# Value loads through one fp32 buffer, one early q/k load from ScalarE's queue, and three pairs' transposes in other PSUM banks

## The chip, the cores and the metric

The kernel runs on one core of a Trainium2 chip. The metric is the time of one execution on the device, in microseconds (us); lower is better. Engines are called PE (TensorE, matmul), DVE (VectorE), ACT (ScalarE), POOL (GpSimd) and SP (SyncE, which here only issues DMAs).

## What is computed

Attention with a window of 96 keys and 8 global keys, an ALiBi bias and softmax, and after it a mixer that adds a low-rank mixing along the sequence and a feed-forward block. Cut to what matters:

```python
scores = q @ k.T / sqrt(D) + bias            # B=4, H=8, S=768, D=64
scores = where(is_global | is_local, scores, -1e9)
a = softmax(scores)
x = concat_heads(a @ v)                      # (4, 768, 512)
h = (x.T @ U @ V).T                          # along the sequence, rank 32
u = x + h
out = u + relu(u @ w_ch1) @ w_ch2            # 512 -> 2048 -> 512
```

## The kernel before, in words

**The tiles.** The heads are worked on in pairs: 4 pairs a batch (`NP` = 4), 16 pairs in all (`NPAIR`), numbered 0 to 15 here. A pair's q, k and v are loaded in fp32 (384 KB each) into the staging tiles qst, kst and vst, two buffers each (L94, L119), cast to fp16 by an engine (`cast_qk`, L108; `cast_v`, L125, on POOL), and used from there. Pairs 0 to 7 (`NPE` = 8) have q and k transposed by PE (`st_T`, L229: twelve 128x128 transposes into two PSUM tiles named tp), and copied out by ACT (two halves of q, into qz) and DVE (k, into kT). Pairs 8 to 15 have them transposed by DMA (`turn`, L308). The rows of pairs 0 to 7 are read from memory in stretches of 1536 bytes (L96), those of the other pairs (L101) and of all values (L120) in stretches of 256 bytes.

**The stages of a pair.** Scores in three chunks (`st_SE` for batch 0, `st_S` after it), exponentials on ACT, the product with the values (`st_V`, once for each head of the pair), whose result DVE divides into x_sb (L427) and POOL casts to fp16, x16 (L428). Then the low-rank mixing: `st_M1` (L437 for batches after the first) multiplies x16 of a pair with U and needs the casts of both heads; `st_MT`, `st_M3` and a DMA transpose (`st_X`, L480) follow.

**Feed-forward.** For each half of a batch there are 16 up units (L526, `mk_up`: four matmuls into a PSUM tile hps, which ACT empties into htr, L530) and down units (L546, `mk_down`: four matmuls each into a tile cps). They stand in two queues, and `fill(n)` puts the next n of them between the attention steps of the pairs, so that PE has work while attention waits. No down unit is placed before the loop's i = 7 (L678, `held`). The first weights w1 come in four chunks (`load_w1`), the second, w2, in four (`load_w2`), issued by POOL, which casts them to fp16 during the DMA.

**PSUM.** Eight banks: tag th (three banks, for hps, tp, ups and tmp_ps), tag cps (two, for the down units; in batch 0 also for scores, and for the output of pair 3's second head), tag sc (two) and tag ob (one). Up unit 0 is begun early in a cps bank (L662).

**Order.** Everything is ordered by hand (`manual_schedule`, L138): each engine does its instructions in the order in which the code gives them, and waits are by semaphore. SP issues all loads but the weights, all stores and all DMA transposes, in one in-order queue; its next DMA waits until the one before it could be issued, and an issue waits until its target buffer is free. Batch 0 is the loop at L615; the rest is the loop at L674, whose pass i does scores of pair i, values and division of pair i-1, and transposes and casts ahead. In the second loop SP's loads stand at L683 to L690: q/k of a later pair, then the values of pair i+1, ahead of the cast of values i (L697) and of `st_A` (L698, which for pairs 8 to 15 issues the two vA DMAs, L289 and L290). On POOL the order in pass 5 is: `cast_v`, `st_A`, w2 chunk 2 (L700), L428 for pair 4's second head, w2 chunk 3 (L708).

**Activation memory.** htr (L523) has two buffers of 128 x 16 x 384 fp16; they are first written when the up units begin, after batch 0.

Of the kernel before, what the change touches and what calls it, by code (L numbers as in the profile page):

```python
# [11 lines left out]
FP32 = mybir.dt.float32  # L12
FP16 = mybir.dt.float16
# [7 lines left out]
def kernel(  # L21
# [13 lines left out]
    nc = tc.nc  # L35
    B, H, S, D = q.shape
    NG = int(n_global)
    NL = int(n_local)
    P = 128
    DM = H * D  # L40
    NSB = S // P
    DFF = moe_w_ch1.shape[1]
    NDC = DM // P
    NJC = DFF // P
    R = moe_U.shape[1]
    NP = H // 2
# [14 lines left out]
    GT = S // 2  # L61
# [4 lines left out]
    stp = ctx.enter_context(tc.tile_pool(name="stp", bufs=2))  # L66
# [4 lines left out]
    ffp = ctx.enter_context(tc.tile_pool(name="ffp", bufs=2))  # L71
    psum = ctx.enter_context(tc.tile_pool(name="psum", bufs=1, space=bass.MemoryType.PSUM))
# [10 lines left out]
    def ps_th(name, dtype=FP32, cols=512):  # L83
        return psum.tile([P, cols], dtype, name=name, tag="th", bufs=3)
# [2 lines left out]
    NVB = 4  # L87
    vbuf = [cst.tile([P, NSB, 2, D + 1], FP16, name=f"v16_{i}") for i in range(NVB)]

    def load_qk(i):  # L90
        b, h0 = i // NP, 2 * (i % NP)
        got = []
        for src, nm in ((q, "qst"), (k, "kst")):
            st = stp.tile([P, 2, NSB, D], FP32, name=nm, tag=nm, bufs=2)  # L94
            if i < NPE:
                nc.sync.dma_start(  # L96
                    st.rearrange("p h n d -> p h (n d)"),
                    src[b, h0:h0 + 2].rearrange("h (p n) d -> p h (n d)", n=NSB),
                )
            else:  # L100
                nc.sync.dma_start(  # L101
                    st.rearrange("p h n d -> p (h n) d"),
                    src[b, h0:h0 + 2].rearrange("h (n p) d -> p (h n) d", p=P),
                )
            got.append(st)
        staged[i] = got
# [9 lines left out]

    def load_v(i):
        b, h0 = i // NP, 2 * (i % NP)
        st = stp.tile([P, 2 * NSB, D], FP32, name="vst", tag="vst", bufs=2)  # L119
        nc.sync.dma_start(  # L120
            st, v[b, h0:h0 + 2].rearrange("h (n p) d -> p (h n) d", p=P)
        )
        vsts[i] = st
# [9 lines left out]
    NPAIR = B * NP  # L133
# [48 lines left out]
    def finish_table(t):  # L182
        nc.gpsimd.tensor_scalar_max(t[0:NG, 0, 0:P], relB[0:NG, 0:P], float(-NL))
        nc.gpsimd.memset(t[0:NG, :, P:], float(-NL))
# [29 lines left out]
    def load_w2(c):  # L214
        nc.gpsimd.dma_start(w2_16[:, 4 * c:4 * c + 4], w2v[:, 4 * c:4 * c + 4])
# [13 lines left out]
    def st_T(i):  # L229
        stq, stk = cast.pop(i)  # L230
        kT = kp.tile([P, S], FP16, name="kT", tag="kT")
        kA = kp.tile([P, NSB - 1, P], FP16, name="kA", tag="kA")
        tps = []
        for st in (stq, stk):

            tp = ps_th("tp", FP16, S)
            tps.append(tp.rearrange("d (n p) -> d p n", n=NSB))
            for n in range(NSB):
                nc.tensor.matmul(
                    tp[:, n * P:(n + 1) * P], st[:, n].rearrange("s h d -> s (h d)"), ident16,  # L240
                    is_transpose=True, start=(n == 0), stop=(n == NSB - 1),
                )
        tq, tk = tps
        z = qz[i % 2]
        if i == 0:
            kts[i], kas[i] = kT, kA
            for a in range(2):
                ts, ps = slice(a * GT, (a + 1) * GT), slice(a * P // 2, (a + 1) * P // 2)
                for hi in range(2):
                    r = slice(hi * D, (hi + 1) * D)  # L250
                    nc.scalar.copy(
                        z[hi][r, ts].rearrange("d (p n) -> d p n", n=NSB), tq[r, ps]
                    )
                nc.vector.tensor_copy(kT[:, ts].rearrange("d (p n) -> d p n", n=NSB), tk[:, ps])
                ns = slice(0, 2) if a == 0 else slice(2, NSB - 1)
                nc.vector.tensor_copy(
                    kA[:, ns].rearrange("d n p -> d (n p)"), kT[:, ns.start * P:ns.stop * P]
                )
                ns = slice(max(1, ns.start), ns.stop)
                nc.vector.tensor_copy(  # L260
                    kA[:, ns, 0:NG],
                    kT[:, 0:NG].unsqueeze(1).broadcast_to((P, ns.stop - ns.start, NG)),
                )
            return
        nc.scalar.copy(z[0][0:D].rearrange("d (p n) -> d p n", n=NSB), tq[0:D])
        nc.vector.tensor_copy(kT.rearrange("d (p n) -> d p n", n=NSB), tk)  # L266
        kts[i], kas[i] = kT, kA
        if i > NP:
            st_KA(i, nc.gpsimd)
        if i <= NP + 1:  # L270
            nc.scalar.copy(z[1][D:P].rearrange("d (p n) -> d p n", n=NSB), tq[D:P])
        else:
            nc.vector.tensor_copy(z[1][D:P].rearrange("d (p n) -> d p n", n=NSB), tq[D:P])

    def st_KA(i, eng):
        kT, kA = kts[i], kas[i]
        eng.tensor_copy(kA.rearrange("d n p -> d (n p)"), kT[:, 0:S - P])
        eng.tensor_copy(  # L278
            kA[:, 1:, 0:NG], kT[:, 0:NG].unsqueeze(1).broadcast_to((P, NSB - 2, NG))
        )  # L280
# [334 lines left out]
    for i in range(NP):  # L615
        st_SE(i, 0)
        if i:
            st_V(i - 1, 0)
        cast_v(i)
        st_A(i)  # L620
        if i < 2:
            load_v(i + 2)
        if i in (1, 2):
            load_qk(NP - 1 + i)
        if i == 2:
            load_w1(0)
        if i == 3:
            load_v(NP)
        if i >= 2:
            st_M1(i - 2)  # L630
        if i:
            st_T(i + 1)
        st_SE(i, 1)
        if i:
            st_V(i - 1, 1)
        else:
            st_T(i + 1)
        st_KA(i + 1, nc.vector)
        st_P(i)
        if i == 2:  # L640
            st_M2(i - 2)
        if i == 0:
            cast_qk(i + 2, nc.vector, nc.gpsimd)
        elif i < 3:
            cast_qk(i + 2, nc.gpsimd)
        if i == 2:
            load_w1(1)
        if i == 3:
            load_w1(2)
            load_w1(3)  # L650
        st_SE(i, 2)
        if i == 3:
            st_M2(i - 2)
# [4 lines left out]
    cast_qk(NP + 1, nc.gpsimd)  # L658
    st_M2(NP - 2)
    nc.scalar.copy(relcat, rel3)  # L660
    finish_table(relcat)
    begin_up(0, (0, 1), ps_cps("hps"))  # L662
    st_M1(NP - 1)
# [10 lines left out]
    for i in range(NP, NPAIR + 2):  # L674
        b, hp = divmod(i, NP)
        live = i < NPAIR
        n = 1 if i < 2 * NP + 1 else 2
        held[0] = i < NP + 3  # L678
        if hp == 0 and live and b + 1 < B:
            new_batch(b + 1)  # L680
        if live and i > NP:
            st_S(i, 0)
        early = {NP: (NP + 2,), NP + 1: (NP + 3,), NP + 2: (NP + 5,)}  # L683
        for j in early.get(i, (i + 3,)):
            if j < NPAIR:
                load_qk(j)
        if i + 1 < NPAIR:
            load_v(i + 1)
        if i == NP + 1:
            load_qk(NP + 4)  # L690
        fill(2)
        if NP < i <= NPAIR:
            st_V(i - 1, 0)
        if i + 1 < NPE:
            st_T(i + 1)
        if live:
            cast_v(i)  # L697
            st_A(i)  # L698
            if i == NP + 1:
                load_w2(2)  # L700
        fill(n)
        if live:
            st_S(i, 1)
        fill(1)
        if NP < i <= NPAIR:
            st_V(i - 1, 1)
        if i == NP + 1:
            load_w2(3)  # L708
        if i > NP + 1 and (i - 2) % NP == NP - 1:
            queue_ff((i - 2) // NP, 0)  # L710
            queue_ff((i - 2) // NP, 1)
            ahead[0] = 1
        if i == NPAIR + 1:
            break
        more = 1 if i + 1 < NPE else 0
        fill(n + more)
        if live:
            st_S(i, 2)
            if i < NPE:
                st_P(i)  # L720
        fill(1)
        if i > NP:
            st_M1(i - 1)
        if NPE <= i + 1 < NPAIR:
            st_Z(i + 1)
        if i + 2 < NPAIR:
            cast_qk(i + 2, nc.gpsimd)
        if i == NP:
            load_w2(0)
            load_w2(1)  # L730
        if live:
            st_E(i, 0)
        fill(1)
        if i > NP:
            st_MT(i - 1)
        if NPE <= i + 1 < NPAIR:
            st_K(i + 1)
        fill(1)
        if i > NP:
            st_M3(i - 1, 0)  # L740
        if live:
            st_E(i, 1)
        fill(1)
        if i > NP:
            st_M3(i - 1, 1)
            st_X(i - 1)
        if i + 2 < NPAIR and i + 2 >= NPE:
            turn(i + 2)
        fill(n - more)
# [38 lines left out]
```

## Time and profile before

| what | value |
|---|---|
| median of 3 runs | 239.45 us (239.22 to 239.78) |
| the profiled execution | 239.77 us |
| its span, first to last instruction | 238.0 us |
| granted TensorE clock | 1.00 |
| PE busy | 227.8 us (96%) |
| DVE, ACT, POOL busy | 130.2, 120.7, 94.9 us |
| HBM read, written | 27.46 MB, 6.29 MB |

How to read it: the profile is of one execution. Each engine's busy time is the sum of its instructions; the idle time before an instruction is put down to whoever ended it. Matmuls are pipelined and overlap, so PE's gaps are best seen from start to start: six 128-column matmuls in a row start about 0.055 us apart, four 384-column ones 0.163 us. The DMA share is that of 16 DMA engines; a DMA is moved as packets, here one for each stretch of memory. The loads' median time from issue to landing is 4.9 us (q), 5.5 (k), 6.1 (v), and 10.8 for a weight chunk.

### The profile page before, as it was taken

The numbers are of one execution on the slowest core, as the hardware profiler recorded it, in microseconds if no ns is written. First come the engines' busy times: TensorE is split into PE (matmuls) and PEld (weight loads), VectorE is DVE, ScalarE is ACT, GpSimd is POOL, SyncE is SP. The second block draws the span as 40 slices with busy tenths as digits, with TensorE's granted clock in tenths as the row PEclk, the third lists the DMA queues.
The fourth block names the chain that finished last, engine by engine and source line by source line (L and its number), as shares of the span: only waits on it lengthen the run. The fifth ranks groups of instructions, "written<-read, shape, count | busy, mean of one in ns | idle before, by whom it ended". The sixth has DMA issues, their size and how long they took to land.

```text
span 238.0 us, 4939 instructions
## 1 busy us (share of the span) xinstructions
PE 227.8 (96%) x1964; PEld 139.2 (59%) x1964; DVE 130.2 (55%) x281; ACT 120.7 (51%) x207; POOL 94.9 (40%) x146
## 2 busy tenths in 40 slices
PE   7889969999999999999999999999999999999994
PEld 2558746757555556666666566666555555555453
DVE  4777656789687786665766775755333111011121
ACT  6989767786741302865544317473632244533200
POOL 8479937576474635455727254513111000000000
PEclk9999999999999999999999999999999999999999
DMA  6999999999978989997969581751211210011022
GB/s 191 308 284 280 240 232 236 245 230 164 212 167 213 221 237 165 254 169 182 214 167 222 170 232 42 204 29 39 69 55 38 85 47 25 19 44 47 13 75 88
DMA packets 86558, 36.61 MB, mean 154 GB/s; under 512 B 74152, under 2 KB 83592, under 8 KB 86536
## 3 DMA queue, kind: packets, MB, share of 16 engines
q1 hardware_dynamic: 81480, 32.01, 56.1%
q0 software_dynamic: 5056, 4.29, 11.5%
q8 instruction: 15, 0.25, 0.4%
q14 instruction: 7, 0.06, 0.1%
HBM read 27.46 MB, written 6.29 MB: 142 GB/s over the span
## 4 chain that ended last, share of the span: by engine, by line
PE 78%; DMA 7%; DVE 5%; POOL 4%; ACT 2%; issue 1%; SPq 1%; POOLq 0%
PE cps L546 33%; PE hps L526 30%; DMA w<-in_moe_w_ch_dram 4%; DMA kst<-in_k_dram 3%; PE sc L349 3%; PE sc L354 2%; PE ob L408 2%; PE cps L564 1%; PE ob L404 1%; DVE kT L266 1%; POOL v L127 1%; DVE x_sb L427 1%; ACT ep L392 1%; PE sc L491 1%; POOL x L428 1%
## 5 line engine op out<-in xcount | busy, mean ns | idle before, releaser
L530 ACT ACTIVATE htr<-hps 128x384 f16<-128x384 f32 x128 | 61.3, 492 | 84.0 <-PE hps L526 83.4
L526 PE MATMUL hps<-uT,w 128*128 128x384 f16 x506 | 97.5, 326 | 0.7 <-DVE uT L473 0.3
L546 PE MATMUL cps<-w,htr 128*128 128x512 f16 x368 | 91.2, 379 | 0.0
L526 PEld LDWEIGHTS <-w 128*128 128x128 f16 x506 | 46.5, 98 | 29.4 <-issue 1.0
L380 DVE SCALAR_TENSOR_TENSOR sp<-sc,relcat 128x512 f32<-128x512 f32 (+1 forms) x72 | 43.2, 640 | 20.2 <-PE sc L354 14.3
L546 PEld LDWEIGHTS <-htr 128*128 128x128 f16 x368 | 34.1, 98 | 31.1
L552 DVE TENSOR_TENSOR osb<-cps,x_sb 128x512 f32<-128x512 f32 x23 | 15.9, 690 | 49.8 <-PE cps L546 49.5
L392 ACT ACTIVATE ep<-sp 128x1408 f16<-128x1408 f32 x24 | 32.7, 1372 | 12.2 <-DVE sp L380 12.2
L428 POOL CAST x<-x_sb 128x384 f16<-128x384 f32 x30 | 15.5, 518 | 49.5 <-DVE x_sb L427 49.4
L349 PE MATMUL sc<-qz,kT 128*128 128x128 f16 x192 | 27.8, 219 | 0.2 <-DVE kT L266 0.2
L354 PE MATMUL sc<-qz,kA 128*128 128x128 f16 x160 | 25.5, 220 | 0.9 <-DVE kA L278 0.3
L349 PEld LDWEIGHTS <-kT 128*128 128x128 f16 x192 | 18.3, 98 | 3.9 <-DVE kT L266 0.5
L354 PEld LDWEIGHTS <-kA 128*128 128x128 f16 x160 | 15.6, 98 | 7.3 <-DVE kA L278 1.1
L500 POOL CAST x<-x_sb 128x768 f16<-128x768 f32 x12 | 9.9, 829 | 21.5 <-DVE x_sb L496 21.5
L427 DVE TENSOR_TENSOR x_sb<-ob,rcp 128x384 f32<-128x384 f32 x30 | 16.7, 557 | 1.0
L408 PE MATMUL ob<-v,ep 128*128 128x65 f16 x192 | 15.8, 193 | 0.0
L408 PEld LDWEIGHTS <-ep 128*128 128x128 f16 x192 | 13.9, 98 | 2.1
L127 POOL CAST v<-vst 128x768 f16<-128x768 f32 x16 | 13.4, 839 | 3.5 <-DMA vst<-in_v_dram 3.5
L323 POOL COPY qz<-qT 64x768 f16<-64x768 f16 x16 | 13.3, 830 | 2.9 <-DMA qT<-q 2.5
L404 PE MATMUL ob<-vA,ep 128*128 128x65 f16 x160 | 14.0, 194 | 0.0
L113 POOL CAST k<-kst 128x768 f16<-128x768 f32 x14 | 12.1, 864 | 1.0 <-ACT ep L367 1.0
L367 ACT ACTIVATE ep<-sc 128x512 f16<-128x512 f32 (+1 forms) x24 | 11.9, 561 | 1.0 <-PE sc L354 0.9
(91 smaller groups left out, 203.0 us busy)
## 6 DMA issues: line engine op xcount, KB each, us to landing
qst<-in_q_dram SPq DMA_DIRECT2D x16, 384.0 KB, 4.9
kst<-in_k_dram SPq DMA_DIRECT2D x16, 384.0 KB, 5.5
vst<-in_v_dram SPq DMA_DIRECT2D x16, 384.0 KB, 6.1
out_dram<-osb SPq DMA_DIRECT2D x23, 256.0 KB, 2.1
w<-in_moe_w_ch_dram POOLq DMA_DIRECT2D x8, 512.0 KB, 10.8
vA<-v SPq DMA_DIRECT2D x8, 152.3 KB, 3.4
out_dram<-osb SPq DMA_DIRECT2D x2, 128.0 KB, 1.7
uT<-x SPq DMA_TRANSPOSE x12, 4.4
```

What stands on the lines that cost most here:

```text
L349: nc.tensor.matmul(sc[:, o:o + P], kT[:, kb * P:(kb + 1) * P], z[:, kb * P:(kb + 1) * P], start=(o == 0 and not on_pe), stop=(o + P == tot),)
L354: nc.tensor.matmul(sc[:, o + P:o + 2 * P], kA[:, kb], z[:, (kb + 1) * P:(kb + 2) * P], start=False, stop=(o + 2 * P == tot),)
L380: nc.vector.scalar_tensor_tensor(out=sps[i, hi][:, c0:c0 + tot], in0=sc[:, 0:tot], scalar=qk_scale / slope[2 * (i % NP) + hi], in1=relf[:, ...
L392: nc.scalar.activation(ep, sps.pop((i, hi)), AF.Exp, scale=slope[2 * (i % NP) + hi])
L404: nc.tensor.matmul(ob[:, qi], ep[:, OF[qi - 1]:OF[qi - 1] + P], vA[:, qi - 1, hi], start=True, stop=False,)
L408: nc.tensor.matmul(ob[:, qi], ep[:, DG[qi]:DG[qi] + P], vt[:, qi, hi], start=(qi == 0), stop=True,)
L427: nc.vector.tensor_tensor(xo, ob[:, :, 0:D], rb, ALU.mult)
L428: nc.gpsimd.tensor_copy(x16, xo)
L526: nc.tensor.matmul(hps[:, 0:GT], w1_16[:, dc, jt * P:(jt + 1) * P], uT[:, dc, ts], start=(dc == 0), stop=(dc == NDC - 1),)
L530: nc.scalar.activation(cell["htr"][:, jt], hps[:, 0:GT], AF.Relu)
L546: nc.tensor.matmul(cps, htr[:, jc, t * P:(t + 1) * P], w2_16[:, jc], start=(b > 0 and jc == 0), stop=(jc == NJC - 1),)
L552: nc.vector.tensor_tensor(osb, cps, x_sb[:, n], ALU.add)
```

## The change

Four things are changed, all in batch 0 and the loop after it.

1. vst has one buffer instead of two. The values of pairs 1 and 3 are loaded into the two htr buffers, seen as fp32. So values 3 need no staging buffer of their own, and from then on each value load has to wait for the cast of the pair before. The loads are moved to match: values 4 go into pass 2 of the first loop (ahead of pair 5's q/k), and in the second loop values i+1 are issued after `cast_v(i)` and `st_A(i)`.
2. Pair 6's q/k are issued by ACT, after the copy of relcat (L660), and not by SP in pass 4. Pairs 7 and 8 are both issued in pass 5.
3. The transposes of pairs 5, 6 and 7 write cps banks instead of th banks. ACT copies both halves of q for all pairs; before, DVE copied the upper half for pairs 6 and 7.
4. w2 chunk 2 is issued beside chunk 3, after L428 of pass 5.

SP's order from pair 4 on, before: pair 4, pair 5, values 4, pair 6, values 5, pair 7, values 6, pair 8. After: pair 4, values 4, pair 5, values 5, pair 7, pair 8, values 6. PE's instructions and their order are the same.

```diff
-    def load_qk(i):
+    def load_qk(i, queue=nc.sync):
...
-                nc.sync.dma_start(
+                queue.dma_start(
...
     def load_v(i):
         b, h0 = i // NP, 2 * (i % NP)
-        st = stp.tile([P, 2 * NSB, D], FP32, name="vst", tag="vst", bufs=2)
+        if i in (1, 3):
+            st = ffp.tile([P, NJC, GT], FP16, name="htr", tag="htr").bitcast(FP32)
+            st = st.rearrange("p j t -> p (j t)")[:, 0:2 * NSB * D].rearrange(
+                "p (n d) -> p n d", d=D
+            )
+        else:
+            st = stp.tile([P, 2 * NSB, D], FP32, name="vst", tag="vst", bufs=1)
...
-            tp = ps_th("tp", FP16, S)
+            tp = ps_th("tp", FP16, S) if i <= NP else psum.tile(
+                [P, 1024], FP16, name="tp", tag="cps", bufs=2
+            )[:, 0:S]
...
-        if i <= NP + 1:
-            nc.scalar.copy(z[1][D:P].rearrange("d (p n) -> d p n", n=NSB), tq[D:P])
-        else:
-            nc.vector.tensor_copy(z[1][D:P].rearrange("d (p n) -> d p n", n=NSB), tq[D:P])
+        nc.scalar.copy(z[1][D:P].rearrange("d (p n) -> d p n", n=NSB), tq[D:P])
...
         st_A(i)
-        if i < 2:
+        if i < 3:
             load_v(i + 2)
         if i in (1, 2):
             load_qk(NP - 1 + i)
...
-        if i == 3:
-            load_v(NP)
...
     nc.scalar.copy(relcat, rel3)
+    load_qk(NP + 2, nc.scalar)
     finish_table(relcat)
...
-        early = {NP: (NP + 2,), NP + 1: (NP + 3,), NP + 2: (NP + 5,)}
+        early = {NP: (), NP + 1: (NP + 3, NP + 4), NP + 2: (NP + 5,)}
         for j in early.get(i, (i + 3,)):
             if j < NPAIR:
                 load_qk(j)
-        if i + 1 < NPAIR:
-            load_v(i + 1)
-        if i == NP + 1:
-            load_qk(NP + 4)
...
             cast_v(i)
             st_A(i)
-            if i == NP + 1:
-                load_w2(2)
+            if i + 1 < NPAIR:
+                load_v(i + 1)
...
         if i == NP + 1:
+            load_w2(2)
             load_w2(3)
```

## The prediction, made before the run

> **What bounds it.** I read the busy shares first (PE is busy for 96% of the span), then the stretches of 10 us, then TensorE's timeline gap by gap, and for each gap the engine and the queue behind it. By stretches (start:end, length, busy us and instructions of PE, weight loads, DVE, ACT, POOL; clock, DMA share, GB/s):
>
> ```profile
> 30.00:40.00 10.00, 7.86 (x71) 5.42 (x72) 6.65 (x14) 6.67 (x15) 4.68 (x9) 1.00 1.20 216
> 40.00:50.00 10.00, 9.37 (x102) 6.51 (x101) 7.32 (x15) 7.95 (x15) 7.02 (x12) 1.00 1.19 248
> 50.00:60.00 10.00, 9.85 (x110) 6.74 (x107) 8.43 (x17) 7.55 (x13) 6.41 (x11) 1.00 1.31 189
> ...
> 70.00:80.00 10.00, 10.00 (x84) 5.57 (x83) 7.83 (x17) 2.00 (x2) 5.15 (x7) 1.00 0.87 207
> ```
>
> From 70 us on PE has no hole to speak of, so a gap opened or closed before that moves the end by its own length. In the same stretches the DMA engines are full (share 1.19 to 1.31). TensorE's timeline names the gaps (start, length, what; in brackets the idle time and who ended it):
>
> ```profile
> 31.46 0.50 PE L509 MATMUL hps<-uT,w 128*128 128x384 f16 x2 [1.46 <-DMA w<-in_moe_w_ch_dram]
> ...
> 44.04 0.49 PE L239 MATMUL tp<-ident,q 128*128 128x128 f16 x6 [0.22 <-ACT htr L530]
> ...
> 49.80 0.31 PE L437 MATMUL ob<-u,x 128*128 128x32 f16 x6 [0.41 <-POOL x L428]
> ...
> 59.96 0.32 PE L437 MATMUL ob<-u,x 128*128 128x32 f16 x6 [0.15 <-POOL x L428]
> ```
>
> A first-layer weight chunk, a bank held by an up unit, and twice a GpSimd cast. Counted from start to start, less the usual spacing, the last three cost 0.38, 0.56 and 0.32 us. GpSimd around the last two:
>
> ```profile
> 48.49 0.74 POOL L215 DMA_DIRECT2D w<-in_moe_w_ch_dram  x1
> 49.23 0.52 POOL L428 CAST x<-x_sb 128x384 f16<-128x384 f32 x1
> ...
> 57.32 0.84 POOL L127 CAST v<-vst 128x768 f16<-128x768 f32 x1
> 58.23 0.73 POOL L286 COPY vA<-v 128x650 f16<-128x650 f16 x1
> 59.39 0.51 POOL L428 CAST x<-x_sb 128x384 f16<-128x384 f32 x1 [0.44 <-DVE x_sb L427]
> ```
>
> The cast that pair 5's M1 waits for (59.39) stands behind the cast of values 6 (57.32). If values 6 are late, TensorE is late, with only 0.44 us of slack on GpSimd. They are issued at 38.72 now, ahead of pair 8:
>
> ```profile
> 38.72 0.37 SPq L120 DMA_DIRECT2D vst<-in_v_dram  x1
> 40.29 2.71 SPq L101 DMA_DIRECT2D qst<-in_q_dram  x1
> 43.09 2.44 SPq L101 DMA_DIRECT2D kst<-in_k_dram  x1
> ```
>
> **The parts, worked out.** All against the profiled execution: 239.77 us, 238.0 of it span, 0.32 over the median of 239.45. PE's instruction order does not change, so only its gaps can.
>
> 1. *Banks for the transposes of pairs 5 to 7.* They leave the three th banks to the up units. Gaps that go: 0.28 (after the transposes, at 35.20) and 0.40 (at 36.70, ended by ACT's qz copy) for pair 5; 0.38, and 0.04 + 0.04 + 0.07 around it, for pair 6; 0.14 at 56.37 for pair 7. But pair 5 meets a new wait: its first cps bank still holds the output of pair 3's second head, which DVE reads last (two L668, 33.78 to 34.79), its second the first up unit (ACT, 34.28 to 34.77). Its transposes start at 34.24 now and would start at about 34.8: 0.55 lost. Pair 5 nets 0.13, pair 6 0.53, pair 7 0.14: **0.8 saved**.
>
> 2. *Upper half of q for pairs 6 and 7 from DVE (0.96 each) to ACT (0.79 by the row of the lower half).* DVE's x_sb (48.36, 58.77) moves up by as much; ACT has idle stretches of 0.23, 0.67 and 0.50 just behind (45.65 to 47.80) and three banks of lead. With part 3 this frees the casts at 49.23 and 59.39: GpSimd would reach them at about 48.5 and 58.9. Gaps 0.56 and 0.32, less what remains, and the 0.2 that DVE costs at L454 (60.97): **1.0 saved**, both parts together.
>
> 3. *Second-layer chunk 2 behind the cast.* Its 0.74 of GpSimd at 48.49 moves behind L428. Without part 2 it alone would give 0.28 (x_sb ends at 48.92, the cast starts at 49.23).
>
> 4. *Pair 6 from ACT.* Two issues after the copy of relcat, which ends at 31.71. No row shows ACT issuing. Nearest: SP's four pair issues from 18.66 to 24.50, 0.37 to 0.42 each; farthest, SP's at 30.08 and 34.35, 4.17 and 1.47. SP's long ones stand behind its own unfinished loads, and ACT's queue is empty, so I take 0.8 in all: free at 32.5, before the next ACT work is ready (33.64, it waits 1.93 for PE). Cost nothing; at 5.64, ACT is free at 37.4 and the first bank of part 1 comes 3.1 us late. Pair 6 needs to land by 39.4. It moves 512 packets of 1536 bytes beside first-layer weights, at the rate that window 31 to 32 us shows (106 of pair 6's beside 108 of the weights' per us): from about 33.5 to 38.4. Just in time, and its users have 2 us to spare (cast ends 41.1, transposed at 44.04).
>
> 5. *First-layer chunk 0, which ends the gap of 1.46 at 31.46.* Pair 6 no longer runs beside it (28 to 30 us: 222 packets each), but pair 5 does, because SP now issues it behind values 4, which wait for GpSimd's cast of values 2 (ends 20.74; pair 5 went at 18.66). At most 1.1 is to be had (after the chunk, M1 of pair 3 waits for ACT's L422, to 30.61), at worst 0.5 is lost. **0.5 saved**, from the middle.
>
> 6. *One fp32 buffer for values.* From pair 4 on each value load waits for the cast of the pair before, and is issued behind it. From values 9 on this is covered: the tightest are values 11, issued at 104.93 (4.7 us to landing) and now behind the 2.2 us of vA's two issues, so landing at about 111.8 for a cast at 112.93. **Values 6 are not covered.** SP's new order is values 5, pair 7, pair 8, values 6; these go after the cast of values 5 (47.76). A queue moves its packets in order, so ahead of them stand pair 8's two loads, 3072 packets of 256 bytes. What beside weights happens to such loads, by queue in window 47 to 48 us (q0 the weights, q1 SP's):
>
> ```profile
> q0 software_dynamic: 159, 0.16, 94.0%
> q1 hardware_dynamic: 142, 0.04, 27.1%
> ```
>
> One packet for one. Alone, SP moved 1902 in 50 to 52 us. In the trace pair 8 is moving from 46.5 and mostly through by 53, when chunks 2 and 3 of the second layer begin (38 packets in 52 to 52.5, 798 in 53 to 57); these are 1024 packets. Values 6, 1536 packets, would start at 53 beside them: at 145 to 150 per us 1024 packets take 6.9 us, the other 512 0.6. They land at about **60**, an estimate from these windows; below, alone behind pair 8, at 55; above, with the last of the weights' landing (60.53) and a straggling engine, 61.5. I take 60, since the traffic of 40 to 60 us is the same set of loads in both kernels and the DMA engines have no idle in it: the last of the set lands at 60.53 now.
>
> Then cast 0.84, vA 0.73, L428 0.51: pair 5's M1 at 62.1 instead of 59.96. **2.15 lost**, and this swallows the savings of parts 1 to 5 that come before it, since M1 now follows the DMA, not PE. Only 0.2 behind it (L454) counts. Sum: 239.77 + 2.15 - 0.2 = 241.7; less 0.32, **241.4**.
>
> [...] The row above, 142 to 159, speaks for even turns.
>
> **Rivals.**
> - *Values 6 in time* (lands by 57): the weights start later, or values 6 get more than an even share. Then the savings stand: 0.8 + 1.0 + 0.5 = 2.3, giving 237.5, or 237.1 against the median; to 236.8 if chunk 0 comes early enough. For it: the weights issued at 48.49 showed almost no packets before 52 (56 in 50 to 52), so a start 2 us later is not far off. Against it: the landings of value loads beside weights, 8.3 and 16.3 us (issued 38.72 and 26.48), against 4.2 alone. Chance 0.3.
> - *Slower by ACT's issues* (part 4 at its far end): up to 3.1 us at pair 5's transposes, everything behind on GpSimd moves along, weights too: 242.9 if values 6 add nothing, 243.5 if they add something. It decides from about 1.1 us of issuing on. Chance 0.06.
> - *The banks do nothing*: pair 5's new wait eats part 1, values 6 half late (58): 239.3 to 239.9. Chance 0.08.
> - *Values 6 late*, the forecast: 240 to 242.9. Chance 0.56.
>
> So faster by over 0.2% (about what a measurement of this kernel can tell from no change) 0.32, within 0.09, slower 0.59. The range, 237.0 to 243.2, holds both signs; the likeliest case alone is 240.0 to 242.9.
>
> **What would show it.** Right: GpSimd's L127 for pair 6 with a DMA wait of 2 us or more, L437 at some 62, value loads in that stretch taking 10 us or more to land; no PE gap before L437 at 49.8; pair 5's transposes at about 34.8 less what chunk 0 gave. Wrong: values 6 landed by 57, or ACT's two issues together over 1 us, or pair 6 landing after 42.

## The result, and the profile after

The changed kernel takes **245.36 us** (median of 6 runs, 244.71 to 246.45), the kernel before 239.53 (6 runs, 239.00 to 240.96): a ratio of 1.0242, 95% interval 1.0205 to 1.0278. The forecast was 241.4, in a range of 237.0 to 243.2: the sign is right, the size is not. The profiled execution took 245.60 us, with a span of 243.5 (before: 239.77 and 238.0), so the two profiles differ by 5.5 us of span. The ratios further down leave out runs more than 1.5% above the fastest of the same kernel, which takes four of e8's ten runs and leaves e7 without a ratio.

First the stretches of the kernel after, with the same columns as before (start:end, length, busy us and instructions of PE, weight loads, DVE, ACT, POOL; clock, DMA share, GB/s):

```profile
30.00:40.00 10.00, 9.24 (x87) 6.37 (x85) 6.51 (x12) 7.76 (x15) 4.60 (x8) 1.00 1.15 238
40.00:50.00 10.00, 9.82 (x114) 6.97 (x111) 7.29 (x16) 9.10 (x16) 8.30 (x13) 1.00 1.14 232
50.00:60.00 10.00, 6.82 (x79) 4.75 (x76) 5.98 (x12) 7.17 (x12) 2.27 (x4) 1.00 1.28 186
60.00:70.00 10.00, 7.27 (x42) 4.46 (x43) 3.39 (x7) 3.12 (x5) 4.46 (x6) 0.66 0.56 127
70.00:80.00 10.00, 9.90 (x94) 5.78 (x92) 8.12 (x17) 3.14 (x3) 6.68 (x9) 1.00 0.87 205
```

Up to 50 us PE is busier than before (9.24 and 9.82 where it was 7.86 and 9.37). Most of the first difference is not the engine edits' work: the first up unit starts at 29.52 instead of 31.46, so its long wait has left this stretch. From 50 to 70 PE stands still for some 6 us. And one column has moved that the prediction never used: the granted clock of the stretch 60 to 70 is 0.66. PE's line of 40 slices and the clock's, on the page of the kernel after, show the same:

```profile
PE   7999989993699999999999999999999999999994
...
PEclk9999999999589999999999999999999999999999
```

The empty slice (3) comes first, the slow ones (5 and 8) right behind it. TensorE's timeline of the kernel after names the gaps (start, length, what; in brackets idle time and who ended it):

```profile
29.52 0.50 PE L514 MATMUL hps<-uT,w 128*128 128x384 f16 x2 [0.46 <-DMA w<-in_moe_w_ch_dram]
...
32.92 0.49 PE L247 MATMUL tp<-ident,q 128*128 128x128 f16 x6 [0.45 <-DVE x_sb L672]
...
47.03 0.32 PE L442 MATMUL ob<-u,x 128*128 128x32 f16 x6 [0.18 <-POOL x L433]
...
56.00 0.81 PE L531 MATMUL hps<-uT,w 128*128 128x384 f16 x4
62.73 0.34 PE L442 MATMUL ob<-u,x 128*128 128x32 f16 x6 [5.92 <-POOL x L433]
...
68.30 0.84 PE L531 MATMUL hps<-uT,w 128*128 128x384 f16 x4
69.19 1.03 PE L551 MATMUL cps<-w,htr 128*128 128x512 f16 x4
```

The gaps at the first up unit (0.46 for 1.46) and at pair 4's M1 (0.18 for 0.41) are smaller, the one at 32.92 is the new wait of pair 5's transposes, and there is one gap of 5.92 before pair 5's M1 (L442, L437 before), which starts at 62.73; before it started at 59.96. GpSimd's timeline there:

```profile
54.32 0.21 POOL L283 COPY kA<-kT 128x32 f16<-128x32 f16 x1
60.59 0.84 POOL L133 CAST v<-vst 128x768 f16<-128x768 f32 x1 [6.06 <-DMA vst<-in_v_dram]
61.49 0.73 POOL L291 COPY vA<-v 128x650 f16<-128x650 f16 x1
62.16 0.51 POOL L433 CAST x<-x_sb 128x384 f16<-128x384 f32 x1
```

This is the same row of casts as before (57.32, 58.23, 59.39), but the first now waits 6.06 us for values 6. The chain of waits through this stretch (start, length) runs from the load to M1 without a branch:

```profile
45.75 14.78 DMA vst<-in_v_dram
60.59 0.85 POOL v L133
61.49 0.73 POOL vA L291
62.22 0.46 POOL x L433
62.73 0.34 PE ob L442 x6
```

The load is issued at 45.75 and takes 14.78 us to land, at 60.53. SP's issues after:

```profile
38.97 0.46 SPq L101 DMA_DIRECT2D qst<-in_q_dram  x1
40.37 2.41 SPq L101 DMA_DIRECT2D kst<-in_k_dram  x1
45.75 1.43 SPq L126 DMA_DIRECT2D vst<-in_v_dram  x1
51.28 7.80 SPq L485 DMA_TRANSPOSE uT<-x  x1
```

Pair 8 (38.97, 40.37) is ahead of the values in the queue. What runs beside them, by queue of the kernel after in window 53 to 57 us (packets, MB, share; q0 the weights, q1 SP's):

```profile
q0 software_dynamic: 718, 0.72, 106.6%
q1 hardware_dynamic: 349, 0.09, 16.3%
```

**Where the 5.5 us are.** Three marks on PE that both kernels have: pair 5's M1, the first down unit, the last matmul. M1: 59.96 before, 62.73 after, **2.77 later**. From M1 to the first down unit: 63.98 - 59.96 = 4.02 before, 69.19 - 62.73 = 6.46 after, **2.44 more** for the same matmuls with no new gap between them. From M1 to the last matmul: 174.47 before, 177.18 after, 2.71 more. So half the loss is M1's delay, and the other half arises behind M1 at once. In the stretch from 61.51 to 68.33, 6.83 us long, the clock is granted at 0.5; PE works in it from 62.73, 5.6 us at half the clock, which is 2.8 lost by estimate (four matmuls of L531 take 1.49 us there, at 64.25, and 0.81 at 56.00, where the clock is 1.00). The first down unit of the kernel before, and that stretch of the kernel after, with the columns of the stretches above:

```profile
63.98 1.03 PE L546 MATMUL cps<-w,htr 128*128 128x512 f16 x4
```

```profile
61.51:68.33 6.82, 5.60 (x34) 3.58 (x35) 2.24 (x6) 2.63 (x4) 2.77 (x4) 0.50 0.63 143
```

### The profile page after: what moved, and what is told of

Its sections match the earlier page's. It is cut to its first block, busy times and chain, and to the rows that moved or that the text cites. A ratio compares the mean times of both kernels' runs of the same rounds, so it can differ in the third digit from the quotient of the medians.

```text
span 243.5 us, 4944 instructions
## 1 busy us (share of the span) xinstructions
PE 229.8 (94%) x1964; PEld 140.7 (58%) x1964; DVE 128.7 (53%) x279; ACT 121.8 (50%) x209; POOL 95.6 (39%) x146
## 4 chain that ended last, share of the span: by engine, by line
PE 77%; DMA 11%; POOL 4%; DVE 4%; ACT 2%; issue 1%; SPq 0%; POOLq 0%
PE cps L551 32%; PE hps L531 29%; DMA vst<-in_v_dram 6%; DMA w<-in_moe_w_ch_dram 4%; PE sc L354 3%; PE sc L359 3%; DMA kst<-in_k_dram 2%; PE ob L413 2%; PE cps L569 1%; POOL v L133 1%; PE ob L409 1%; PE tp L247 1%; ACT ep L397 1%; PE sc L496 1%; POOL vA L291 1%
## 5 line engine op out<-in xcount | busy, mean ns | idle before, releaser
L531 PE MATMUL hps<-uT,w 128*128 128x384 f16 x506 | 99.3, 331 | 0.3 <-DVE uT L478 0.3
L531 PEld LDWEIGHTS <-w 128*128 128x128 f16 x506 | 46.9, 99 | 29.5 <-issue 1.6
L433 POOL CAST x<-x_sb 128x384 f16<-128x384 f32 x30 | 15.6, 518 | 48.2 <-DVE x_sb L432 48.2
L505 POOL CAST x<-x_sb 128x768 f16<-128x768 f32 x12 | 10.0, 829 | 24.4 <-DVE x_sb L501 24.4
L133 POOL CAST v<-vst 128x768 f16<-128x768 f32 x14 | 12.0, 860 | 8.1 <-DMA vst<-in_v_dram 8.1
L413 PEld LDWEIGHTS <-ep 128*128 128x128 f16 x192 | 13.9, 98 | 2.1
L113 POOL CAST k<-kst 128x768 f16<-128x768 f32 x14 | 12.7, 905 | 1.8 <-DMA kst<-in_k_dram 1.2
L409 PEld LDWEIGHTS <-ep 128*128 128x128 f16 x160 | 10.9, 97 | 2.1
```

The lines of the kernel that those rows point to most:

```text
L409: nc.tensor.matmul(ob[:, qi], ep[:, OF[qi - 1]:OF[qi - 1] + P], vA[:, qi - 1, hi], start=True, stop=False,)
L413: nc.tensor.matmul(ob[:, qi], ep[:, DG[qi]:DG[qi] + P], vt[:, qi, hi], start=(qi == 0), stop=True,)
L433: nc.gpsimd.tensor_copy(x16, xo)
L531: nc.tensor.matmul(hps[:, 0:GT], w1_16[:, dc, jt * P:(jt + 1) * P], uT[:, dc, ts], start=(dc == 0), stop=(dc == NDC - 1),)
```

## The experiments

**The theory** after reading the traces: (a) values 6 are late because they stand behind pair 8 in SP's queue, and move beside the second-layer weights; (b) the gap that this opens on PE makes the clock fall, and the slow stretch behind it costs as much again. **Rivals**: the single buffer is what makes values late (the issue waits for a buffer); the other parts of the change cost something too; the second half of the loss is work that has become longer, not the clock.

| kernel | median, us | ratio to before, 95% | idle of PE before M1 of pair 5 / 6, and half-clock time, in the profile, us |
|---|---|---|---|
| e1_values_first | 240.91 | 1.0069 (1.0027 to 1.0111) | none / 2.38; 3.41 |
| e2_weights_later | 239.40 | 1.0017 (0.9978 to 1.0055) | 1.29 / 1.11; 0 |
| e3_pe_kept_busy | 243.60 | 1.0185 (1.0123 to 1.0247) | filled / none; 0 |
| e4_two_buffers | 244.55 | 1.0221 (1.0148 to 1.0294) | 5.01 / none; 6.83 |
| e5_both_values_first | 238.70 | 0.9982 (0.9939 to 1.0026) | none / none; 0 |
| e6_loads_as_before | 238.57 | 0.9981 (0.9954 to 1.0009) | none / 1.89; 3.41 |
| e7_loads_alone | 246.09 | none (4 runs, 242.08 to 246.45) | 5.25 / none; 6.83 |
| e8_no_load_moved | 238.40 | 0.9943 (0.9901 to 0.9986) | none / 2.60; 0 |
| e9_values_7_early | 237.95 | 0.9963 (0.9930 to 0.9997) | none / none; 0 |
| e10_and_pair_6_scalar | 238.76 | 0.9998 (0.9971 to 1.0025) | none / none; 0 |
| e11_pe_half_busy | 244.31 | 1.0238 (1.0187 to 1.0288) | 3.94 / none; 3.41 |
| e12_banks_as_before | 238.30 | 0.9964 (0.9934 to 0.9995) | none / none; 0 |

The kernel before took 239.08 beside e1 to e8 and 238.81 beside e9 to e12. The profile of e6 is of the only one of its eleven runs with a mean clock below 0.999 (242.10 us).

### Is it the order in the queue, the weights, or the buffer?

**e1_values_first**: the kernel after, with pair 8 issued behind values 6.

```diff
-        early = {NP: (), NP + 1: (NP + 3, NP + 4), NP + 2: (NP + 5,)}
+        early = {NP: (), NP + 1: (NP + 3,), NP + 2: (NP + 5,)}
...
             if i + 1 < NPAIR:
                 load_v(i + 1)
+            if i == NP + 1:
+                load_qk(NP + 4)
```

> The changed kernel, but SP issues values 6 ahead of pair 8's two loads; the single buffer and its wait for the cast of values 5 stay. Queue theory (values 6 are late because they stand behind pair 8's 3072 packets beside the last two second-layer chunks): values 6 land by about 51, GpSimd does not wait for them, the 6.1 us gap at pair 5's M1 goes and with it the stretch of half clock, so 245.4 falls by 6.0 + 2.8 to about 236.6. Buffer theory (one buffer is too few, whatever the order): values 6 still wait for the cast of values 5 and stay late, over 243.

Values 6 are no longer late, but values 7 now are. GpSimd's two casts in e1:

```profile
54.77 0.84 POOL L133 CAST v<-vst 128x768 f16<-128x768 f32 x1
...
66.72 0.84 POOL L133 CAST v<-vst 128x768 f16<-128x768 f32 x1 [3.20 <-DMA vst<-in_v_dram]
```

The first has no wait left: the order in the queue decides. But the time of 240.91 is above the expected 236.6, because the next pair meets the same fate. Values 7 are issued at 61.44, behind pair 9, and PE waits before the next M1:

```profile
68.86 0.34 PE L442 MATMUL ob<-u,x 128*128 128x32 f16 x6 [2.38 <-POOL x L433]
```

**e2_weights_later**: the kernel after, with w2 chunks 2 and 3 issued one pass later.

```diff
         if i == NP + 1:
-            load_w2(2)
-            load_w2(3)
...
             if i + 1 < NPAIR:
                 load_v(i + 1)
+            if i == NP + 2:
+                load_w2(2)
+                load_w2(3)
```

> The changed kernel, but second-layer chunks 2 and 3 are issued behind the cast of values 6 and its vA copy in pass 6. Queue theory with even turns: values 6, still behind pair 8 but with no weights beside them, land at about 55; GpSimd waits about 1 us, the clock stays full, some 237 to 238.5, with perhaps 1 to 2 us more where the down units now wait for the late weights. If the weights have no part in it (values 6 late by the queue order alone): no change, 245.

With the same order in SP's queue as in the kernel after, values 6 are in time: their cast in e2 starts without a wait.

```profile
55.98 0.84 POOL L133 CAST v<-vst 128x768 f16<-128x768 f32 x1
```

In the window of 53 to 57 us SP's queue moves 2578 packets beside 8 of the weights, where the kernel after moved 349 beside 718:

```profile
q1 hardware_dynamic: 2578, 0.65, 89.7%
q0 software_dynamic: 8, 0.01, 0.9%
```

So it takes both: the place behind pair 8 and the weights beside it. The time is not better than before, since three smaller gaps are left (1.29, 1.18 and 1.11 us in the profile, ending at 59.61, 69.47 and 71.60): the cast L433 now stands behind the weights' issues, the down units wait for the late weights, and values 7 are late. The profiled run took 242.18 us, 2.8 over the median, so its gaps are read for their causes and not added up.

**e4_two_buffers**: the kernel after with a second buffer for vst.

```diff
-            st = stp.tile([P, 2 * NSB, D], FP32, name="vst", tag="vst", bufs=1)
+            st = stp.tile([P, 2 * NSB, D], FP32, name="vst", tag="vst", bufs=2)
```

> The changed kernel with two fp32 buffers for values again, all orders unchanged: values 6 no longer wait for the cast of values 5, but still stand behind pair 8 on SP's queue. Queue theory: values 6 are issued some 3 us earlier and land when they did, about 60: 245. Buffer theory: values 6 in time, 236 to 238.

Values 6 are issued 2.4 us earlier (43.34) and cast at the same time (60.60; 60.59 in the kernel after), M1 starts at 62.75.

```profile
60.60 0.84 POOL L133 CAST v<-vst 128x768 f16<-128x768 f32 x1 [5.16 <-DMA vst<-in_v_dram]
```

The first rival falls: the buffer is not what makes values 6 late. Their place in the queue is.

**e7_loads_alone**: the kernel before with the moved loads and the one buffer alone (the transposes' banks, the copies and w2 chunk 2 as before), and **e6_loads_as_before**: the reverse, the kernel after with the loads of values and of pairs 7 and 8 where they were, and two buffers. Both diffs are against the kernel after; e7:

```diff
-            tp = ps_th("tp", FP16, S) if i <= NP else psum.tile(
-                [P, 1024], FP16, name="tp", tag="cps", bufs=2
-            )[:, 0:S]
+            tp = ps_th("tp", FP16, S)
...
-        nc.scalar.copy(z[1][D:P].rearrange("d (p n) -> d p n", n=NSB), tq[D:P])
+        if i <= NP + 1:
+            nc.scalar.copy(z[1][D:P].rearrange("d (p n) -> d p n", n=NSB), tq[D:P])
+        else:
+            nc.vector.tensor_copy(z[1][D:P].rearrange("d (p n) -> d p n", n=NSB), tq[D:P])
...
             st_A(i)
+            if i == NP + 1:
+                load_w2(2)
...
         if i == NP + 1:
-            load_w2(2)
             load_w2(3)
```

> The kernel before with the moved loads alone (one fp32 buffer, two early ones in htr, the new order, pair 6 from ScalarE); banks, the upper halves of q on VectorE and chunk 2's place as before. Queue theory: values 6 land at about 60.5 whatever the engines do; pair 5's M1 at 62.7 as in the changed kernel, from a start 1.5 us later, so a gap of some 4 us and the clock falls again: 244 to 246. If the lateness came from the faster engines alone: 239 to 240.

And e6:

```diff
-        if i in (1, 3):
...
-            st = stp.tile([P, 2 * NSB, D], FP32, name="vst", tag="vst", bufs=1)
+        st = stp.tile([P, 2 * NSB, D], FP32, name="vst", tag="vst", bufs=2)
...
-        early = {NP: (), NP + 1: (NP + 3, NP + 4), NP + 2: (NP + 5,)}
+        early = {NP: (), NP + 1: (NP + 3,), NP + 2: (NP + 5,)}
...
+        if i + 1 < NPAIR:
+            load_v(i + 1)
+        if i == NP + 1:
+            load_qk(NP + 4)
         fill(2)
```

> The changed kernel without part 6 of the prediction: values through two fp32 buffers, all value loads in the places of the kernel before, pair 8 behind values 6; banks, ScalarE's copies, chunk 2's place and pair 6 from ScalarE stay. If the prediction's parts 1 to 5 are right (2.3 saved): 236.8 against 239.1. If values 7 (issued at 60.7 in the kernel before, in a stretch full of DMA) are the next to be late: between 237.5 and 239.

The loads alone give 246.09, everything but the loads 238.57, before is 239.08. The whole loss is the loads', and the second rival falls as far as this loss goes. The clock is to be seen in e7's times too: its one run with a mean clock of 1.00 took 242.08, the other three, at 0.984 to 0.986, took 245.96 to 246.45. That is more than the 2.66 us which e3 gives for the clock, so the gap may have been shorter in that run as well; it was not profiled.

### Is the second half of the loss the clock?

**e3_pe_kept_busy**: the kernel after with 28 extra matmuls of 512 columns, whose result nothing uses, ahead of pair 5's M1; **e11_pe_half_busy**: the same with 14 (the diff is e3's).

```diff
+        if i == NP + 2:
+            warm(28)
         if i > NP:
             st_M1(i - 1)
```

> The changed kernel with 28 extra 128x512 matmuls of zeros (6.0 us) on TensorE just ahead of pair 5's M1, in a free bank; their result is not used. They fill the gap while GpSimd waits. Clock theory (the idle 6 us let the granted clock fall to 0.5 for 6.8 us, of which TensorE worked 5.6, costing 2.8): clock 1.00 throughout, M1 still at about 62.7, 242.6. Without that theory (only the gap costs): 245.4, or more.

> e3 with 14 extra matmuls (3.0 us) in place of 28: TensorE then idles for about 3 us ahead of pair 5's M1 in place of 6, at the same end of the gap. Clock theory with a window of some 3.4 us (the half-clock stretches were 6.8 and 3.4 us long): the clock falls in some runs, for 3.4 us and not 6.8, so 1.0 to 1.5 over e3's 243.6 less its overrun of 0.7, 243 to 244.5, or 242.9 where it does not fall. If idle time is paid by its length alone: 242.9 in all runs. If any long gap costs the same: 245.4.

TensorE's timeline of e3:

```profile
57.79 6.21 PE L160 MATMUL warm<-zw 128*128 128x512 f16 x28
63.84 0.30 PE L442 MATMUL ob<-u,x 128*128 128x32 f16 x6
...
67.64 1.03 PE L551 MATMUL cps<-w,htr 128*128 128x512 f16 x4
```

and its stretches from there:

```profile
60.00:64.00 4.00, 4.00 (x26) 1.88 (x25) 0.56 (x1) 0.00 (x0) 2.93 (x5) 1.00 1.01 215
64.00:68.00 4.00, 4.00 (x40) 2.69 (x37) 2.51 (x6) 2.95 (x5) 1.48 (x2) 1.00 0.46 105
```

GpSimd waits as in the kernel after (5.33 us for values 6), M1 comes even later (63.84, since the extra matmuls outlast the cast by 0.7), and yet the kernel is faster: 243.60 against 245.36. The clock stays at 1.00, and from M1 to the first down unit it is 67.64 - 63.84 = 3.80 us, not 6.46. The fall of the clock costs **2.66 us** of this stretch. That is theory (b), and the third rival falls: the same work takes the old time at the full clock. The expected 242.6 was missed by 1.0, and M1 came 1.1 later than in the kernel after.

e11 leaves 3.94 us of the gap open. Its window in the profile, with the same columns:

```profile
64.00:67.40 3.40, 2.98 (x17) 1.64 (x18) 0.99 (x3) 0.49 (x1) 1.96 (x3) 0.50 0.98 221
```

One stretch of 3.41 us at half clock, half of the kernel after's 6.83. Two of its six runs kept a mean clock of 0.998 or more (243.30 and 243.40), four were at 0.993 (244.19 to 246.21). So a shorter gap is punished less, and not in every run.

Gaps and half-clock time in the profiles, together: 5.92 (after), 5.25 (e7) and 5.01 us (e4) gave 6.83 us; 3.94 (e11), 2.38 (e1) and 1.89 (e6) gave 3.41; 2.60 (e8) and 1.29 (e2) gave none. The length of a gap alone does not sort these cases; its place in time does. The clock changes on a grid: in each trace with several changes they lie whole multiples of 3.413 us apart (in the kernel after at 61.51, at 68.33, two steps on, and at 242.41, 51 steps on, when the matmuls are done; in e1 at 68.49, 71.90 and 239.15, one and 49 steps on). The table has the step of 3.41 us that ends where the clock falls, and the steps that hold a gap where it doesn't; in e8 and e2, whose clock changes only once the matmuls are done, they are counted back from that change (at 236.93 and 240.15).

| kernel (gaps) | steps, us from the start | PE busy in them, us | clock right behind |
|---|---|---|---|
| after (5.92) | 58.09 to 61.51 | 0.00 | 0.50 |
| e7 (5.25) | 58.94 to 62.36 | 0.18 | 0.50 |
| e4 (5.01) | 58.12 to 61.53 | 0.00 | 0.50 |
| e11 (3.94) | 60.59 to 64.00 | 0.00 | 0.50 |
| e1 (2.38) | 65.07 to 68.49 | 1.41 | 0.50 |
| e6 (1.89) | 67.09 to 70.50 | 1.52 | 0.50 |
| e8 (2.60) | 62.85 to 66.26; 66.26 to 69.68 | 2.65; 1.58 | 1.00; 1.00 |
| e2 (1.18, 1.11) | 66.07 to 69.49; 69.49 to 72.90 | 2.24; 2.30 | 1.00; 1.00 |

So the clock fell behind steps in which PE had worked for 1.52 us or less, and stayed behind those with 1.58 or more. An edge of some 1.5 us in 3.41 is an estimate from this table, since the ends of matmuls are modelled. e6's gap of 1.89 lies whole in one step; e8's longer one is split by a boundary and leaves enough work in both. The length of the slow time goes with the same count, at another edge (between 2.20 and 2.99): PE worked 2.19 us (after), 2.20 (e4) and 1.41 (e7) in the first slow step, and a second followed; it worked 2.99 (e11), 3.04 (e1) and 3.41 (e6), and none did. The grid lies differently from run to run (a step begins 0.07 us after the first instruction in the kernel after, 2.56 in e11), which would explain why e8 and e11 lost the clock in some of their runs only. That is not shown run by run, and no run set the place of a gap in the grid on purpose.

A step did not have to be idle for the clock to fall: in e1 and e6 PE worked 1.41 and 1.52 us in it. Nor did the gap have to be as long as a step: it was 2.38 and 1.89 us there.

### What is left when values 6 are in time

**e5_both_values_first**: e1, with pair 9 also issued behind values 7.

```diff
-        early = {NP: (), NP + 1: (NP + 3,), NP + 2: (NP + 5,)}
+        early = {NP: (), NP + 1: (NP + 3,), NP + 2: ()}
...
-            if i == NP + 1:
-                load_qk(NP + 4)
+            if i in (NP + 1, NP + 2):
+                load_qk(i + 3)
```

> As e1, and values 7 too are issued ahead of their pair (pair 9), behind the cast of values 6. In e1 GpSimd waited 3.2 us for values 7, TensorE 2.6 at pair 6's M1, and the clock fell for 3.4 us. Queue theory: values 7 go at about 59.9, right behind the DMA transpose, instead of 61.4 behind 3072 packets, and land at about 64; the gap at pair 6's M1 shrinks to under 1 us and the clock stays full: 240.2 for e1's middle falls by 3 to about 237. Buffer theory (the wait for the cast of values 6, not the order): values 7 late as in e1, 240.

238.70, M1 of both pairs without a gap and the clock at 1.00; compared with e1 that is 2.2 us. It stops near the time of before, and pair 9 is now the late one: two gaps of 0.60 and 0.67 us behind its transposed q, at 70.5 and 71.5.

**e8_no_load_moved**: the kernel before with three engine edits alone: the banks, the q copies on ACT, and w2 chunk 2 beside chunk 3.

```diff
-            tp = ps_th("tp", FP16, S)
+            tp = ps_th("tp", FP16, S) if i <= NP else psum.tile(
+                [P, 1024], FP16, name="tp", tag="cps", bufs=2
+            )[:, 0:S]
...
-        if i <= NP + 1:
-            nc.scalar.copy(z[1][D:P].rearrange("d (p n) -> d p n", n=NSB), tq[D:P])
-        else:
-            nc.vector.tensor_copy(z[1][D:P].rearrange("d (p n) -> d p n", n=NSB), tq[D:P])
+        nc.scalar.copy(z[1][D:P].rearrange("d (p n) -> d p n", n=NSB), tq[D:P])
...
-            if i == NP + 1:
-                load_w2(2)
...
         if i == NP + 1:
+            load_w2(2)
             load_w2(3)
```

> The kernel before with the three engine edits alone (banks, ScalarE's copies, chunk 2 behind the cast); no load moved. By parts 1 to 3 of the prediction 1.8 is saved: 237.3 against 239.1. If values 7 bind next: 238 to 239.

It has values 7 late: GpSimd's cast waits 3.42 us and PE 2.60 before pair 6's M1.

```profile
65.96 0.84 POOL L127 CAST v<-vst 128x768 f16<-128x768 f32 x1 [3.42 <-DMA vst<-in_v_dram]
```

In this profile the clock did not fall; in four of its ten runs it did (0.993), and those took 240.79 to 241.94 where the others took 236.80 to 238.67. The difference of some 3 us is more than half of 3.41 us at half speed; whether the gap was longer in those runs too stays open, since none of them was profiled.

**e9_values_7_early**: e8, with values 7 issued in pass 5, behind values 5's cast and st_A, and so ahead of pair 9.

```diff
-        if i + 1 < NPAIR:
+        if i + 1 < NPAIR and i != NP + 2:
             load_v(i + 1)
...
             cast_v(i)
             st_A(i)
+            if i == NP + 1:
+                load_v(NP + 3)
```

> e8 (the three engine edits on the kernel before, two fp32 buffers) and values 7 issued one pass earlier, behind pair 8 and the cast of values 5, ahead of the DMA transpose. Queue theory: in e8 GpSimd waited 3.4 us for values 7 and TensorE 2.8; issued at about 47 they land by about 61, the gap at pair 6's M1 goes, and with it the half-clock stretch of the runs in which that gap set it off (e8 ran at 236.8 to 238.7 or 240.8 to 241.9): 235.5 to 236.5, with a narrow spread. If values 7 land as late as before since the stretch is full of DMA anyway: as e8, 238.4.

All twelve runs lie between 236.25 and 239.72, with a mean clock of 0.999 or 1.00. The cast and M1 of pair 6 in e9 wait for nothing:

```profile
63.27 0.84 POOL L127 CAST v<-vst 128x768 f16<-128x768 f32 x1
```

```profile
66.13 0.30 PE L436 MATMUL ob<-u,x 128*128 128x32 f16 x6
```

It beats both kernels: 237.95 us, 0.9963 of before, though the interval (0.9930 to 0.9997) only just leaves out no gain. The forecast of e9 itself, 235.5 to 236.5, was too good.

### What the other parts are worth

**e10_and_pair_6_scalar**: e9, with pair 6 issued by ACT as in the change.

```diff
     nc.scalar.copy(relcat, rel3)
+    load_qk(NP + 2, nc.scalar)
...
-        early = {NP: (NP + 2,), NP + 1: (NP + 3,), NP + 2: (NP + 5,)}
+        early = {NP: (), NP + 1: (NP + 3,), NP + 2: (NP + 5,)}
```

> e9 and pair 6 issued by ScalarE as in the changed kernel (part 4 of the prediction alone). If it frees first-layer chunk 0: TensorE's gap ahead of up unit 0 shrinks by up to 1.0 and the time by as much, 235 to 235.5. If pair 6 then lands late: its cast waits 1 to 3 us on GpSimd, a gap at pair 6's transposes, e9's time or more, 236 to 237.

It takes 238.76, 0.8 more than e9, run beside it (by the means of twelve runs each 1.0, 95% interval 0.4 to 1.7). In e10 pair 6's k is late, and PE waits for its cast:

```profile
42.77 0.83 POOL L113 CAST k<-kst 128x768 f16<-128x768 f32 x1 [2.37 <-DMA kst<-in_k_dram]
```

```profile
43.66 0.51 PE L241 MATMUL tp<-ident,k 128*128 128x128 f16 x6 [0.90 <-POOL k L113]
```

**e12_banks_as_before**: e9 without the banks.

```diff
-            tp = ps_th("tp", FP16, S) if i <= NP else psum.tile(
-                [P, 1024], FP16, name="tp", tag="cps", bufs=2
-            )[:, 0:S]
+            tp = ps_th("tp", FP16, S)
```

> e9 without the banks (part 1 of the prediction: transposes of pairs 5 to 7 in th banks again). By the prediction the banks are worth 0.8: 0.8 over e9, with the gaps of 0.28, 0.40 and 0.38 of the kernel before back and the wait of 0.6 at pair 5's transposes gone. If ScalarE's copies or chunk 2's place did it all: e9's time.

238.30 against 237.95; by the means of twelve runs each the difference is 0.5, with a 95% interval of -0.2 to 1.2, so the times exclude neither the expected 0.8 nor nothing. The profiles say more: the gaps of 0.29, 0.40, 0.39 and three of 0.07, 0.14 and 0.20 are back, 1.49 together, but pair 5's wait for its cps bank (0.58) is gone, and so are 0.35 ahead of pair 4's M1 and 0.17 behind pair 5's. That leaves some 0.4 us.

## Why the prediction was wrong, point by point

**The failed step** is the end of part 6, "pair 5's M1 at 62.1 instead of 59.96. **2.15 lost**", and under it the rule of its first section that a gap opened before 70 us "moves the end by its own length". The delay of M1 was nearly right (62.73, so 2.77 late). What the step left out is that the gap on PE is not 2.15 us long. The prediction itself said that the savings of parts 1 to 5 are swallowed before M1; swallowed means that PE arrives early and stands idle for them as well. PE came to its last matmul before M1 at 56.49, 2.99 us ahead of before (1.94 of it already at the first up unit, 29.52 against 31.46), and stood for 6.1 us. In this gap a whole step of 3.41 us passed without a matmul, the clock fell for 6.83 us, and that cost 2.7 us more (e3). 2.15 forecast, 0.6 more of delay and 2.7 of clock are the 5.5.

- **Values 6 late: right, and the landing time in part by luck.** The cast waited 6.06 us (at least 2 was named), M1 came at 62.73 (some 62), the load took 14.78 us to land (at least 10). The landing at 60.53 lies in the 55 to 61.5 given. The causes were right (pair 8 ahead, weights beside: e1 and e2), but two terms were off and offset each other. The rate was too favourable: values and weights were to share one for one, at 145 to 150 packets per us each, and from 53 to 57 it was 349 to 718, that is 87 to 180 per us. The start was too late: 53 is when pair 8 was through in the kernel before, where values 6 went ahead of it. Counted in order in the trace of the kernel after, the last of pair 8's 256-byte packets started at 51.0, half of values 6 by 52.2, the last at 58.0. What held the landing until 60.53 is not shown.
- **Banks, 0.8: probably too much.** Pair 5's new wait came as worked out (0.61 us start to start, DVE's L672; forecast 0.55), and the old gaps went, but the net is some 0.4 by the profiles of e9 and e12; their times leave it open.
- **q copies on ACT and chunk 2 behind the cast, 1.0: partly.** They were not tried apart. With the banks they are worth 0.6% by e8's ratio, some 1.4 us, but 0.7 us by its median over all ten runs, and 0.4%, 0.9 us, in e9, which moves values 7 as well; 1.8 was forecast for the three. Of pair 4's M1 gap 0.35 us is left instead of 0.56.
- **Chunk 0, 0.5: not the change's.** The gap at 31.46 shrank from 1.46 to 0.46, but it is as small in e8 and e12, which leave pair 6 on SP, and 1.24 in e2, which has it on ACT. It is not tied to where pair 6 is issued.
- **ACT's issues cost nothing: right for the change, wrong by itself.** They took 0.43 and 0.37 us, at 29.24 and 29.84. Pair 6's k landed at 39.46, and its cast waited 1.19, with no gap on PE. "Just in time" was too thin a cover for another order of loads: in e10 the same move costs 0.8.
- **One buffer, covered from values 9 on: right.** From 70 us the two kernels run alike (0.27 us apart between the first down unit and the last matmul). With two buffers nothing is gained (e4).
- **The rival "values 6 in time" at 237.1** was priced too well. Of the 2.3 us that it counted as saved, e6 shows 0.5, e5 0.4 and e9 0.9, each against the kernel before that ran beside it; in e6 and e1 values 7, the same transfer of the next pass, came late in turn.
- **No rival had the clock in it.** The granted clock stood in the stretches that the prediction shows, as 1.00 in each row: in the kernel before no gap was longer than 1.46 us, and in the step of the grid that holds it PE still worked for 1.98 of 3.41 us. A column that does not move in the kernel before is not a constant of the kernel after.

## What to carry to other kernels

Work out the whole length of a gap on PE, from where PE runs dry to where it starts again, as well as how much later its end comes: savings ahead of a late transfer turn into idle time (here PE came 2.99 us earlier and stood for 6.1), and gaps of 1.9 us and more, all but one of 2.60, halved the clock here for 3.41 or 6.83 us in the profiled runs. When a load is moved behind others, count the packets ahead of it in its own queue and those of the other queues beside it; a free buffer and an issue 2.4 us earlier did not help here (e4, cast at 60.60 instead of 60.59). And when one late transfer is mended, look at the same transfer of the next pass before the gain is counted: here values 7 took the place of values 6.

## What the runs showed of the hardware

- While the kernel had matmuls left, the half-clock time came in two lengths only, 3.41 and 6.83 us, on a grid of 3.413 us. It began behind steps with 1.52 us of PE work or less; a step with 1.58 us in e8 did not set it off.
- An SP issue of a DMA transpose stood for 7.80 us (51.28 to 59.08) in the kernel after, and 7.72 in e1, while loads issued ahead of it on the same queue were under way. In e4 the transpose took 2.54, and single load issues of SP stood for 4.26 in e1 (at 47.80) and 4.96 in e9 (at 45.69), so a long wait is not the transpose's alone. That it is for the loads under way was not tried by itself, nor was it for SP's 4.17 at 30.08 in the kernel before.
- ACT issued its two loads in 0.43 and 0.37 us, as briefly as SP its four pair issues from 18.66 to 24.50 in the kernel before (0.37 to 0.42).
- Where their sizes tell them apart, SP's loads moved in the order of their issues, with some overlap: in the kernel after the middle packet of values 4 (256 bytes, issued at 19.83) started at 21.7, that of pair 5 (1536 bytes, issued at 20.29 and 20.99) at 24.4, that of values 5 (256 bytes, 36.79) at 39.1, that of pair 7 (1536 bytes, 37.25 and 38.45) at 41.3. For pair 8 and values 6, both of 256 bytes, the order is shown by e1 alone, where values 6 go first and their cast has no wait (6.06 us in the kernel after).
- SP's queue of 256-byte packets did poorly beside weight packets of 1 KB in one window of the kernel after, 349 to 718 in 4 us, so 0.09 MB beside 0.72 MB, and about one for one in one of the kernel before (142 to 159 in 1 us); all but alone, it moved 2578 in 4 us (e2).
